# Weight fetches in eight paced pieces, first keys on another queue, and a new order of constants, in a fused attention and expert kernel

## The chip, the cores and the metric

The kernel runs on one core of a Trainium2 chip. The metric is the device time of one execution in microseconds (us): the median of the runs. A profile of one execution stands beside it, with a span of 499.8 us.

## What is computed

```
attention, batch 8, heads 12, sequence 448, head size 64:
  e    = exp(q k^T / 8 - max)
  attn = e / (sum(e) + exp(-max) + 1e-9)          # softmax with a one more in the sum
  x    = (attn v), laid out as 3584 tokens x 768
router, 8 experts: cosine of each token with each expert's embedding / tau
  expert = argmax, gate = softmax weight of that expert
expert MLP, per token:  out = gate * ( relu(x @ w1[expert]) @ w2[expert] )
  w1: 8 x 768 x 1024, w2: 8 x 1024 x 768, float32
```

## The kernel before, in words

The work is one long software pipeline, written out in `pipeline` (from L627). It counts in **steps**: step g (0 to 47) handles one pair of heads, six steps make one batch element b, and each step is cut into 8 slots (`NSLOT`). `put(slot, fn)` files a piece of work under a slot, and at the end all are emitted in order of slot. TensorE keeps this order exactly. On the other engines a scheduler places instructions by the order in which it expects their inputs, and the helper `behind(k, inst, other)` can tell it that one instruction has to come after another in the same engine's queue, which adds no semaphore.

For a pair of heads: queries and keys are loaded (`load_qk`, L166 to L171) and values too (`load_v`, L180 to L182), one group of twelve transfers on SyncE's queue for two steps, into three rotating sets of buffers. `front_q` and `front_k` transpose them on TensorE; VectorE copies the queries (L225), ScalarE the keys (L237). `front_v` (L246 to L254) puts the values into `vab` on GpSimd. `scores` multiplies (L268), takes the exponential on ScalarE (L273) and subtracts 1 on VectorE (L275). `attend` and `attend_rest` (L293, L306) multiply by the values; with them come the sums of the rows, which after every second step ScalarE's queue copies with a small transfer to the tile `den` (L317). `recip` inverts them, GpSimd spreads them over a tile with the constant `chunk` (L339), `normalise` brings them to all rows by a product with the constant `sel` (L350) and writes x.

After the six steps of a batch element the router runs. `router_pick` finds the expert with most tokens of this batch element and GpSimd loads its number into a register. `fetch` then loads that expert's weights, float32 in memory and bf16 in the tile, in four transfers from GpSimd's queue (L476), two halves of w1 and two of w2, from the pool `wp` with six buffers. Some four steps later `moe_chunks` spreads the expert's products over six steps: eight `moe_h` (L488), then seven of `moe_y` and `moe_yr` (L503, L518). Tokens that chose another expert are done in a loop at the end, if there are any.

Before the pipeline `build_consts` makes the constants that the first steps need. `build_late_consts`, in slot 2, makes `sel`, `chunk` (128 x 448, by eight selections on GpSimd, L98), an iota for the router and others. `warm` keeps TensorE busy with 48 products at the start, and with single ones in the first steps.

Buffers and semaphores: a buffer of a pool is filled again when its last reader is done. Each transfer of the SyncE and ScalarE queues signals its end on one of eight semaphores in turn, in the order the scheduler expects, and the program makes a transfer wait until the transfer eight earlier, which used the same semaphore, has landed.

Of the kernel before, what the change touches and what calls it, by code (L numbers as in the profile page):

```python
# [9 lines left out]
F32 = mybir.dt.float32  # L10
# [13 lines left out]
SM = 384  # L24
# [13 lines left out]
def build_consts(k):  # L38
    nc, pool = k.nc, k.const
    k.ident = pool.tile([128, 128], F32, name="ident")  # L40
    make_identity(nc, k.ident[:])
    k.ones_f = pool.tile([128, 1], F32, name="ones_f")
    nc.vector.memset(k.ones_f[:], 1.0)

    k.vld, k.krest, k.qrest, k.vab, k.rc, k.vst = [], [], [], [], [], []
    for s in range(NG):
        v = pool.tile([128, 2 * GP, 4, DH], F32, name=f"vld{s}")
        nc.gpsimd.memset(v[64:128, :, 3, :], 0.0)
        k.vld.append(v)
        kr = pool.tile([128, GP, 128], F32, name=f"krest{s}")  # L50
        nc.vector.memset(kr[:], 0.0)
        k.krest.append(kr)
        qr = pool.tile([128, 2 * GP, DH], F32, name=f"qrest{s}")
        nc.gpsimd.memset(qr[64:128, GP:, :], 0.0)
        k.qrest.append(qr)
    for s in range(2):
        va = pool.tile([128, 4, 4, 64], F32R, name=f"vab{s}")
        for h in range(2):
            nc.vector.tensor_copy(
                out=va[:, :, 2 * h + 1, :],  # L60
                in_=k.ones_f[:, 0:1].unsqueeze(2).broadcast_to([128, 4, 64]),
            )
        k.vab.append(va)
        rc = pool.tile([128, CN], F32R, name=f"rc{s}")
        nc.vector.memset(rc[:].bitcast(F32), 0.0)
        k.rc.append(rc)
        k.vst.append(pool.tile([128, NG, 4 * GP], F32, name=f"vst{s}"))


def build_late_consts(k):  # L70

    nc, pool = k.nc, k.const
    k.ones32 = pool.tile([128, 32], F32, name="ones32")
    nc.vector.memset(k.ones32[:], 1.0)
    k.ones_b = pool.tile([128, 128], BF16, name="ones_b")
    nc.vector.memset(k.ones_b[:], 1.0)


    sel_f = k.yp.tile([128, GP, 2, 64], F32, name="sel_f", tag="y")
    k.chunk = pool.tile([128, CH, CN], BF16, name="chunk")  # L80
    nc.gpsimd.memset(sel_f[:], 0.0)
    nc.vector.memset(k.chunk[:], 0.0)
    for base in (0, 64):
        r = sel_f[base : base + 2 * GP * CH]

        nc.gpsimd.affine_select(out=r, in_=r, compare_op=ALU.is_ge, fill=1.0, base=-1,
                                pattern=[[0, GP], [0, 2], [0, 64]], channel_multiplier=0)
        nc.gpsimd.affine_select(out=r, in_=r, compare_op=ALU.is_ge, fill=0.0, base=0,
                                pattern=[[-2 * CH, GP], [-CH, 2], [0, 64]], channel_multiplier=1)
        nc.gpsimd.affine_select(out=r, in_=r, compare_op=ALU.is_ge, fill=0.0, base=CH - 1,  # L90
                                pattern=[[2 * CH, GP], [CH, 2], [0, 64]], channel_multiplier=-1)
    k.sel = pool.tile([128, GP, 128], F32R, name="sel")
    nc.vector.tensor_copy(out=k.sel[:], in_=sel_f[:].rearrange("p g h d -> p g (h d)"))
    n = 2 * GP * CH
    for base in (0, 64):
        r = k.chunk[base : base + n]
        for i in range(2 * GP):
            nc.gpsimd.affine_select(out=r, in_=r, compare_op=ALU.not_equal, fill=1.0, base=-CH * i,  # L98
                                    pattern=[[-1, CH], [0, CN]], channel_multiplier=1)

    k.mask = pool.tile([128, 4, E], F32, name="mask")
    nc.vector.memset(k.mask[:], 1.0)
    nc.vector.memset(k.mask[64:128, 3, :], 0.0)
    k.ind = pool.tile([128, 4, 32], F32, name="ind")
    for i in range(4):
        nc.vector.reduce_sum(out=k.ind[:, i, :], in_=k.ident[:].rearrange("p (b c) -> p c b", c=32), axis=AX.X)
    k.half = pool.tile([128, 4], F32, name="half")
    nc.vector.memset(k.half[:], 0.5)
    iota_i = pool.tile([128, E], I32, name="iota_i")
    nc.gpsimd.iota(iota_i[:], pattern=[[1, E]], base=0, channel_multiplier=0)  # L110
    k.iota = pool.tile([128, E], F32, name="iota")
    nc.vector.tensor_copy(out=k.iota[:], in_=iota_i[:])
    k.rr = pool.tile([128, 512], F32, name="rr")
    nc.vector.memset(k.rr[:], 0.0)
    k.cnt_all = pool.tile([128, B, E], F32, name="cnt_all")
    k.oh0_all = pool.tile([128, B, E], F32, name="oh0_all")
    k.g_all = pool.tile([128, B, 4, E], F32, name="g_all")
    k.idx_all = pool.tile([128, B, 8], U32, name="idx_all")
# [32 lines left out]
def load_qk(k, n):  # L151
# [9 lines left out]
    def rest2(src, two):  # L161
        return src[b].rearrange("(g two) s d -> two s g d", two=2)[two, SM:S, g0 : g0 + GP, :]

    for dst, src in ((t.qm, k.q), (t.km, k.k)):
        for j in range(3):
            nc.sync.dma_start(  # L166
                dst[:, j, :, :], src[b, h0 : h0 + 2 * GP, 0:SM, :].rearrange("h (p t) d -> t p h d", t=3)[j]
            )
    nc.sync.dma_start(t.qr[0:64, :, :], k.q[b, h0 : h0 + 2 * GP, SM:S, :].rearrange("h p d -> p h d"))
    nc.sync.dma_start(t.kr[0:64, :, 0:64], rest2(k.k, 0))  # L170
    nc.sync.dma_start(t.kr[64:128, :, 64:128], rest2(k.k, 1))  # L171
    k.ld[n] = t


# [66 lines left out]
def front_v(k, g):  # L241
# [3 lines left out]
    for h in range(2):  # L245
# [5 lines left out]
        out=va[0:64, 3, 0, :], in0=t.v[0:64, 2 * i, 3, :],  # L251
        scalar1=1.0, scalar2=0.0, op0=ALU.mult, op1=ALU.add,
    )
    nc.gpsimd.tensor_scalar(  # L254
        out=va[64:128, 3, 2, :], in0=t.qr[64:128, i, :],
        scalar1=1.0, scalar2=0.0, op0=ALU.mult, op1=ALU.add,
    )
# [206 lines left out]
    k.e0[b], k.wts[b] = e0, ([], [])  # L464


def fetch(k, b, i):

    nc, e0 = k.nc, k.e0[b]
    if i < 2:  # L470
        w = k.wp.tile([128, NP, F // 2], BF16, name="w", tag="w")
        src = k.w1[bass.ds(e0, 1), :, :].rearrange("o (c p) f -> p (o c) f", p=128)[:, :, F // 2 * i : F // 2 * (i + 1)]
    else:
        w = k.wp.tile([128, 4, DM], BF16, name="w", tag="w")
        src = k.w2[bass.ds(e0, 1), :, :].rearrange("o (f p) m -> p (o f) m", p=128)[:, 4 * (i - 2) : 4 * i - 4, :]
    nc.gpsimd.dma_start(w[:], src)  # L476
    k.wts[b][i // 2].append(w)


def keep_xb(k, b):  # L480
# [3 lines left out]
def moe_h(k, xb, w1, f):  # L484
    nc = k.nc
    ps = k.work.tile([128, 512], F32, name="work", tag="work")
    for c in range(NP):
        nc.tensor.matmul(  # L488
            ps[:, 0:S], lhsT=w1[f // 4][:, c, 128 * (f % 4) : 128 * (f % 4) + 128], rhs=xb[:, c, :],
            start=(c == 0), stop=(c == NP - 1),  # L490
        )
    h = k.hp.tile([128, S], BF16, name="h", tag="h")
    nc.scalar.activation(h[:], ps[:, 0:S], ACT.Relu)  # L493
    return h


def moe_y(k, hs, w2, g0, t, n):
# [3 lines left out]
    ps = k.work.tile([128, 512], F32, name="work", tag="work")  # L501
    for f in range(NF):
        nc.tensor.matmul(  # L503
            ps[:, 0:SM], lhsT=hs[f][:, 128 * t : 128 * t + 128], rhs=w2[f // 4][:, f % 4, SM * n : SM * n + SM],
            start=(f == 0), stop=(f == NF - 1),
        )
    nc.vector.tensor_scalar_mul(yt[:], ps[:, 0:SM], g0[:, t : t + 1])  # L507
# [3 lines left out]
def moe_yr(k, hs, w2, g0):  # L511
# [4 lines left out]
    for f in range(NF):  # L516
        for n in range(2):
            nc.tensor.matmul(  # L518
                ps[64 * n : 64 * n + 64, 0:SM], lhsT=hs[f][:, SM:S], rhs=w2[f // 4][:, f % 4, SM * n : SM * n + SM],
                start=(f == 0), stop=(f == NF - 1),  # L520
            )
    nc.vector.tensor_scalar_mul(yt[:], ps[:, 0:SM], g0[:, 3:4])
# [29 lines left out]
def other_experts(k):  # L552
# [13 lines left out]
    with tc.If(any_ > 0):  # L566
# [6 lines left out]
        with tc.For_i(0, B * E, 1) as i:  # L573
# [3 lines left out]
            with tc.If(n > 0):  # L577
# [3 lines left out]
                g = p.tile([128, 4], F32, name="gx", tag="gx")  # L581
                nc.sync.dma_start(g[:], k.g_dram.rearrange("b e p t -> (b e) p t")[bass.ds(i, 1)].rearrange("o p t -> p (o t)"))
                nc.vector.tensor_copy(out=g[64:128, 3:4], in_=g[0:64, 3:4])
                w1, w2 = [], []
                for j in range(2):
                    w = k.wp.tile([128, NP, F // 2], BF16, name="w", tag="w")
                    nc.gpsimd.dma_start(
                        w[:],
                        k.w1[bass.ds(e, 1), :, :].rearrange("o (c p) f -> p (o c) f", p=128)[:, :, F // 2 * j : F // 2 * (j + 1)],
                    )  # L590
                    w1.append(w)
                for j in range(2):
                    w = k.wp.tile([128, 4, DM], BF16, name="w", tag="w")
                    nc.gpsimd.dma_start(
                        w[:], k.w2[bass.ds(e, 1), :, :].rearrange("o (f p) m -> p (o f) m", p=128)[:, 4 * j : 4 * j + 4, :]
                    )
                    w2.append(w)
                hs = [moe_h(k, xb, w1, f) for f in range(NF)]
                r0 = b * S
                for t in range(3):  # L600
# [28 lines left out]
def pipeline(k):  # L629
# [4 lines left out]
    def put(slot, fn):  # L634
        at.setdefault(slot, []).append(fn)

    put(2, lambda: build_late_consts(k))
    put(12, lambda: prep_expert_emb(k, k.emb, k.tau))
    put(5 * NSLOT, lambda: prep_expert_emb_t(k))
    for n in range(NG * B):  # L640
# [26 lines left out]
    for b in range(B):  # L667
# [1 line left out]
        put(s, lambda b=b: router_mm(k, b))  # L669
        put(s + 4, lambda b=b: router_tok(k, b))  # L670
        put(s + 7.6, lambda b=b: router_pick(k, b))
        for i, o in enumerate((7.6, 7.6, 9, 18)):
            put(s + o, lambda b=b, i=i: fetch(k, b, i))
        put(s + 14, lambda b=b: keep_xb(k, b))
        put(s + 9, lambda b=b: router_exp(k, b))
        put(s + 14, lambda b=b: router_act(k, b))
# [12 lines left out]
def kernel(  # L689
# [39 lines left out]
    n.xbp = pool("xbp", 3)  # L729
    n.rp = pool("rp", 1)  # L730
    n.g0p = pool("g0p", 3)
    n.wp = pool("wp", 6)
    n.hp = pool("hp", 10)
    n.yp = pool("yp", 3)
    n.ld, n.qts, n.kts, n.ems, n.nbs, n.den, n.va, n.sv = {}, {}, {}, {}, {}, {}, {}, {}
# [40 lines left out]
```

The softmax here doesn't subtract the row's maximum and nothing guards it: scores larger than these inputs give would overflow.

## Time and profile before

| | |
|---|---|
| time, median of 2 runs | 504.06 us (503.33 to 504.8) |
| span of the profiled run | 499.8 us |
| TensorE busy (matmul) | 407.9 us, 82% |
| VectorE, ScalarE, GpSimd busy | 324.1, 273.6, 198.5 us |
| weights transfers | 32 of 768 KB, 13.6 us from issue to landing (median) |
| all transfers | 76.24 MB |

How to read it. The page cuts the span into 40 slices of 12.5 us; each digit is a busy share in tenths. PEclk is the granted clock of TensorE, 9 for full. The share of the transfer engines can exceed 1 in the stage tables[...]. A line of the timeline gives the start, the duration, the engine, the source line, the operation and its tiles, how many were merged, and in brackets how long the engine had been idle and what ended it. SPq and ACTq are the queues of SyncE and ScalarE while they issue transfers. Where several things were waited for, the profile names the one that came last.

### The profile page before, as it was taken

The page shows a single profiled execution, that of the slowest core. Times are in us where ns is not written, and L with a number is a line of the kernel's source. Part 1 is how long each engine was busy: PE and PEld are TensorE (multiplying, and loading weights), DVE is VectorE, ACT ScalarE, POOL GpSimd, SP SyncE. Part 2 cuts the span into 40 slices and gives each one's busy share as a digit, 9 for nine tenths or more (in the row PEclk, how much of TensorE's full clock was granted, in tenths as well). Part 3 has the DMA queues.
Part 4 walks back from the last instruction along what each step waited for, and adds up shares of the span by engine and source line. Part 5 has one row for each costly group of instructions (what it writes and reads, how often), then busy time and mean ns, then how long its engine had stood idle before and what let it go on. Part 6 is the DMA issues. An engine that isn't in the chain of part 4 may idle for free.

```text
span 499.8 us, 7648 instructions
## 1 busy us (share of the span) xinstructions
PE 407.9 (82%) x2392; PEld 248.7 (50%) x2392; DVE 324.1 (65%) x810; ACT 273.6 (55%) x419; POOL 198.5 (40%) x365
## 2 busy tenths in 40 slices
PE   6378688764999399975999399975999499979986
PEld 4245454433566265643565265643565265543533
DVE  3267688893698376874688376874698386864203
ACT  1277476753786267843786267843786277713130
POOL 5665344563356125443356225443356232401200
PEclk9698789995999789997999789997999799999989
DMA  6844436499529956698729966698729911891983
GB/s 158 185 113 114 115 77 194 71 198 220 143 46 195 220 162 170 101 201 222 210 44 192 223 162 168 103 200 214 217 46 194 205 64 57 133 230 59 174 190 112
DMA packets 144204, 76.24 MB, mean 153 GB/s; under 512 B 103193, under 2 KB 143129, under 8 KB 144161
## 3 DMA queue, kind: packets, MB, share of 16 engines
q1 hardware_dynamic: 120336, 44.87, 38.3%
q0 software_dynamic: 22144, 30.67, 32.8%
q10 hardware_dynamic: 1680, 0.17, 0.3%
q8 instruction: 20, 0.33, 0.3%
q14 instruction: 24, 0.19, 0.1%
HBM read 84.17 MB, written 16.52 MB: 201 GB/s over the span
## 4 chain that ended last, share of the span: by engine, by line
PE 56%; DMA 22%; DVE 5%; POOL 5%; ACT 4%; issue 4%; SPq 2%; ACTq 1%; POOLq 0%; DVEq 0%
PE work L488 12%; PE big L293 11%; DMA vld<-in_v_dram 7%; DMA den<-nb 6%; PE work L503 6%; PE big L268 6%; PE work L380 4%; DMA qrest<-in_q_dram 4%; PE big L306 3%; ACT e L273 3%; PE work L222 3%; PE work L350 2%; DMA out_dram<-y 2%; PE work L518 2%; PE work L234 2%
## 5 line engine op out<-in xcount | busy, mean ns | idle before, releaser
L273 ACT ACTIVATE e<-big 128x896 f32<-128x896 f32 x144 | 128.2, 920 | 25.8 <-PE big L268 20.9
L275 DVE TENSOR_SCALAR em<-e 128x896 fp32r<-128x896 f32 x144 | 94.9, 659 | 36.9 <-ACT e L273 35.9
L268 PE MATMUL big<-qt,kt 64*128 64x448 f32 x288 | 54.5, 431 | 60.0 <-ACT kt L237 48.6
L488 PE MATMUL work<-xb,w 128*128 128x448 bf16 x384 | 85.2, 363 | 2.4 <-DVE y L507 2.4
L293 PE MATMUL big<-em,vab 128*128 128x448 f32 x288 | 76.5, 404 | 6.8 <-ACT e L273 5.3
L246 POOL TENSOR_SCALAR vab<-vld 128x192 fp32r<-128x192 f32 x96 | 38.6, 416 | 107.5 <-PE big L293 99.8
L313 ACT COPY nb<-big 128x896 f32<-128x896 f32 x48 | 43.5, 906 | 58.7 <-PE big L306 58.7
L503 PE MATMUL work<-w,h 128*128 128x384 bf16 x384 | 74.4, 345 | 0.1
L507 DVE TENSOR_SCALAR y<-work,g 128x384 f32<-128x384 f32 x48 | 29.4, 612 | 64.7 <-DMA out_dram<-y 42.5
L355 DVE SCALAR_TENSOR_TENSOR x<-nb,sv,work 64x448 f32<-64x448 f32 x96 | 64.9, 676 | 5.0 <-PE work L350 3.4
L293 PEld LDWEIGHTS big<-em,vab 128*128 128x128 f32 x288 | 57.7, 205 | 15.7 <-ACT e L273 6.8
L237 ACT CAST kt<-work 128x512 fp32r<-128x512 f32 x48 | 28.2, 588 | 67.5 <-DMA vld<-in_v_dram 38.5
L268 PEld LDWEIGHTS big<-qt,kt 64*128 64x128 f32 x288 | 25.8, 204 | 74.9 <-ACT kt L237 52.3
L488 PEld LDWEIGHTS <-w 128*128 128x128 bf16 x384 | 35.7, 101 | 39.4 <-issue 15.1
L493 ACT ACTIVATE h<-work 128x448 bf16<-128x448 f32 x64 | 34.9, 545 | 36.4 <-PE work L488 36.2
L503 PEld LDWEIGHTS <-h 128*128 128x128 bf16 x384 | 38.0, 102 | 30.7 <-issue 11.6
L191 POOL TENSOR_TENSOR vs<-vld 128x256 f32<-128x256 f32 x24 | 18.7, 780 | 66.5 <-DMA vld<-in_v_dram 57.1
L225 DVE CAST qt<-work 128x448 fp32r<-128x448 f32 x48 | 29.9, 623 | 15.4 <-PE work L223 14.7
L476 POOL DMA_DIRECT2D w<-in_moe_w_dram x32 | 26.6, 841 | 30.9 <-DVE x L355 25.8
L339 POOL TENSOR_TENSOR rt<-rc,chunk 128x448 fp32r<-128x448 f32 x24 | 25.2, 1049 | 34.4 <-DVE rc L337 32.9
L282 DVE TENSOR_SCALAR emx<-e 128x448 fp32r<-128x448 f32 x48 | 21.5, 447 | 14.0 <-ACT e L280 13.8
L350 PE MATMUL work<-rt,sel 128*128 128x448 f32 x48 | 22.3, 464 | 9.3 <-POOL rt L339 5.9
(113 smaller groups left out, 581.3 us busy)
## 6 DMA issues: line engine op xcount, KB each, us to landing
w<-in_moe_w_dram POOLq DMA_DIRECT2D x32, 768.0 KB, 13.6
qm<-in_q_dram SPq DMA_DIRECT2D x72, 128.0 KB
km<-in_k_dram SPq DMA_DIRECT2D x72, 128.0 KB
vld<-in_v_dram SPq DMA_DIRECT2D x24, 384.0 KB
out_dram<-y SPq DMA_DIRECT2D x48, 192.0 KB
xb_dram<-xb POOLq DMA_DIRECT2D x8, 672.0 KB, 5.3
qrest<-in_q_dram SPq DMA_DIRECT2D x24, 64.0 KB
krest<-in_k_dram SPq DMA_DIRECT2D x48, 32.0 KB
```

The lines of the kernel that those rows point to most:

```text
L225: nc.vector.tensor_copy(out=qt[:], in_=ps[:, 0:S])
L246: nc.gpsimd.tensor_scalar(out=va[:, 0:3, 2 * h, :], in0=t.v[:, 2 * i + h, 0:3, :], scalar1=1.0, scalar2=0.0, op0=ALU.mult, op1=ALU.add,)
L268: nc.tensor.matmul(ps[:, h, 0:S], lhsT=kt[64 * h : 64 * h + 64, 128 * j : 128 * j + 128], rhs=qt[64 * h : 64 * h + 64, :], start=True, sto ...
L273: k.last_e = nc.scalar.activation(e[:], ps[:, :, 0:S], ACT.Exp, scale=scale)
L275: k.last = nc.vector.tensor_scalar_sub(em[:], e[:], 1.0)
L293: nc.tensor.matmul(ps[:, h, 0:S], lhsT=va[:, j, 2 * h : 2 * h + 2, :], rhs=k.ems[g, j][:, h, :], start=(j == 0), stop=False,)
L313: nc.scalar.copy(out=nb[:, i, :, :], in_=ps[:, :, 0:S])
L350: nc.tensor.matmul(ps[:, 0:S], lhsT=k.sel[:, g % GP, :], rhs=rt[:].rearrange("p c n -> p (c n)"), start=True, stop=True)
L355: nc.vector.scalar_tensor_tensor(out=x[r, :], in0=nb[0:64, g % GP, h, :], scalar=k.sv[b][:, 2 * c + h : 2 * c + h + 1], in1=ps[r, 0:S], op ...
L488: nc.tensor.matmul(ps[:, 0:S], lhsT=w1[f // 4][:, c, 128 * (f % 4) : 128 * (f % 4) + 128], rhs=xb[:, c, :], start=(c == 0), stop=(c == NP ...
L493: nc.scalar.activation(h[:], ps[:, 0:S], ACT.Relu)
L503: nc.tensor.matmul(ps[:, 0:SM], lhsT=hs[f][:, 128 * t : 128 * t + 128], rhs=w2[f // 4][:, f % 4, SM * n : SM * n + SM], start=(f == 0), st ...
```

## The change

Three things are changed. The weights of a batch element are fetched in eight pieces of half the size, and each piece is put, by `behind`, after the last `front_v` instruction of its step in GpSimd's queue (`k.last_v`), over six steps; the pool gets ten buffers of half the size. This is meant to spread the transfers over time. The keys of the very first group of heads are loaded through ScalarE's queue beside the queries on SyncE's. The late constants are emitted one slot later, iota is made early, `chunk` is first built narrow and then widened by VectorE, and the copies of `sel` and `chunk` on VectorE are put behind the first scores; this is meant to let the first steps begin before the constants are made.

```diff
 def build_consts(k):
+    iota_i = pool.tile([128, E], I32, name="iota_i")
+    nc.gpsimd.iota(iota_i[:], pattern=[[1, E]], base=0, channel_multiplier=0)
+    k.iota = pool.tile([128, E], F32, name="iota")
+    nc.vector.tensor_copy(out=k.iota[:], in_=iota_i[:])
...
 def build_late_consts(k):
-    k.chunk = pool.tile([128, CH, CN], BF16, name="chunk")
+    ch_f = k.yp.tile([128, CH], F32, name="ch_f", tag="y")
-    nc.vector.memset(k.chunk[:], 0.0)
+    nc.gpsimd.memset(ch_f[:], 0.0)
...
-    nc.vector.tensor_copy(out=k.sel[:], in_=sel_f[:].rearrange("p g h d -> p g (h d)"))
+    behind(k, nc.vector.tensor_copy(out=k.sel[:], in_=sel_f[:].rearrange("p g h d -> p g (h d)")), k.last)
...
-                                    pattern=[[-1, CH], [0, CN]], channel_multiplier=1)
+                                    pattern=[[-1, CH]], channel_multiplier=1)
+    k.chunk = pool.tile([128, CH, CN], BF16, name="chunk")
+    behind(k, nc.vector.tensor_copy(out=k.chunk[:], in_=ch_f[:].unsqueeze(2).broadcast_to([128, CH, CN])), k.last)
...
-    iota_i = pool.tile([128, E], I32, name="iota_i")
-    nc.gpsimd.iota(iota_i[:], pattern=[[1, E]], base=0, channel_multiplier=0)
-    k.iota = pool.tile([128, E], F32, name="iota")
-    nc.vector.tensor_copy(out=k.iota[:], in_=iota_i[:])
...
 def load_qk(k, n):
-    for dst, src in ((t.qm, k.q), (t.km, k.k)):
+    keng = nc.sync if n else nc.scalar
+    for eng, dst, src in ((nc.sync, t.qm, k.q), (keng, t.km, k.k)):
         for j in range(3):
-            nc.sync.dma_start(
+            eng.dma_start(
...
-    nc.sync.dma_start(t.kr[0:64, :, 0:64], rest2(k.k, 0))
-    nc.sync.dma_start(t.kr[64:128, :, 64:128], rest2(k.k, 1))
+    keng.dma_start(t.kr[0:64, :, 0:64], rest2(k.k, 0))
+    keng.dma_start(t.kr[64:128, :, 64:128], rest2(k.k, 1))
...
 def front_v(k, g):
-    nc.gpsimd.tensor_scalar(
+    k.last_v = nc.gpsimd.tensor_scalar(
...
+def w_piece(k, e0, i):
+    if i < 4:
+        w = k.wp.tile([128, NP, F // 4], BF16, name="w", tag="w")
+        src = k.w1[bass.ds(e0, 1), :, :].rearrange("o (c p) f -> p (o c) f", p=128)[:, :, F // 4 * i : F // 4 * (i + 1)]
+    else:
+        w = k.wp.tile([128, 2, DM], BF16, name="w", tag="w")
+        src = k.w2[bass.ds(e0, 1), :, :].rearrange("o (f p) m -> p (o f) m", p=128)[:, 2 * i - 8 : 2 * i - 6, :]
+    return w, k.nc.gpsimd.dma_start(w[:], src)
+
 def fetch(k, b, i):
-    if i < 2:
-        w = k.wp.tile([128, NP, F // 2], BF16, name="w", tag="w")
...
-    nc.gpsimd.dma_start(w[:], src)
-    k.wts[b][i // 2].append(w)
+    w, inst = w_piece(k, k.e0[b], i)
+    behind(k, inst, k.last_v)
+    k.wts[b][i // 4].append(w)
...
 def pipeline(k):
-    put(2, lambda: build_late_consts(k))
+    put(3, lambda: build_late_consts(k))
...
-        for i, o in enumerate((7.6, 7.6, 9, 18)):
-            put(s + o, lambda b=b, i=i: fetch(k, b, i))
+        for i, o in enumerate((1, 1, 2, 3, 4, 4, 5, 6)):
+            put(((b + 1) * NP + 3 + o) * NSLOT + 7.7, lambda b=b, i=i: fetch(k, b, i))
...
-    n.wp = pool("wp", 6)
+    n.wp = pool("wp", 10)
```

`moe_h`, `moe_y` and `moe_yr` take the pieces by new indices (`w1[f // 2]`, `w2[f // 2]`), and the loop at the end uses `w_piece` too.

More of the change, by code (lines that the diff above doesn't have):

```diff
@@ L92, in build_late_consts @@
     k.sel = pool.tile([128, GP, 128], F32R, name="sel")
-    nc.vector.tensor_copy(out=k.sel[:], in_=sel_f[:].rearrange("p g h d -> p g (h d)"))
+    behind(k, nc.vector.tensor_copy(out=k.sel[:], in_=sel_f[:].rearrange("p g h d -> p g (h d)")), k.last)
     n = 2 * GP * CH
     for base in (0, 64):
-        r = k.chunk[base : base + n]
+        r = ch_f[base : base + n]
         for i in range(2 * GP):
             nc.gpsimd.affine_select(out=r, in_=r, compare_op=ALU.not_equal, fill=1.0, base=-CH * i,
-                                    pattern=[[-1, CH], [0, CN]], channel_multiplier=1)
+                                    pattern=[[-1, CH]], channel_multiplier=1)
+    k.chunk = pool.tile([128, CH, CN], BF16, name="chunk")
+    behind(k, nc.vector.tensor_copy(out=k.chunk[:], in_=ch_f[:].unsqueeze(2).broadcast_to([128, CH, CN])), k.last)
     k.mask = pool.tile([128, 4, E], F32, name="mask")
@@ L464, in router_pick @@
     k.e0[b], k.wts[b] = e0, ([], [])
-def fetch(k, b, i):
-    nc, e0 = k.nc, k.e0[b]
-    if i < 2:
-        w = k.wp.tile([128, NP, F // 2], BF16, name="w", tag="w")
[L472 to L475, printed above, removed]
-    nc.gpsimd.dma_start(w[:], src)
-    k.wts[b][i // 2].append(w)
+def w_piece(k, e0, i):
[6 more added lines that the diff above has]
+    return w, k.nc.gpsimd.dma_start(w[:], src)
+def fetch(k, b, i):
+    w, inst = w_piece(k, k.e0[b], i)
+    behind(k, inst, k.last_v)
+    k.wts[b][i // 4].append(w)
 def keep_xb(k, b):
@@ L488, in moe_h @@
         nc.tensor.matmul(
-            ps[:, 0:S], lhsT=w1[f // 4][:, c, 128 * (f % 4) : 128 * (f % 4) + 128], rhs=xb[:, c, :],
+            ps[:, 0:S], lhsT=w1[f // 2][:, c, 128 * (f % 2) : 128 * (f % 2) + 128], rhs=xb[:, c, :],
             start=(c == 0), stop=(c == NP - 1),
@@ L503, in moe_y @@
         nc.tensor.matmul(
-            ps[:, 0:SM], lhsT=hs[f][:, 128 * t : 128 * t + 128], rhs=w2[f // 4][:, f % 4, SM * n : SM * n + SM],
+            ps[:, 0:SM], lhsT=hs[f][:, 128 * t : 128 * t + 128], rhs=w2[f // 2][:, f % 2, SM * n : SM * n + SM],
             start=(f == 0), stop=(f == NF - 1),
@@ L518, in moe_yr @@
             nc.tensor.matmul(
-                ps[64 * n : 64 * n + 64, 0:SM], lhsT=hs[f][:, SM:S], rhs=w2[f // 4][:, f % 4, SM * n : SM * n + SM],
+                ps[64 * n : 64 * n + 64, 0:SM], lhsT=hs[f][:, SM:S], rhs=w2[f // 2][:, f % 2, SM * n : SM * n + SM],
                 start=(f == 0), stop=(f == NF - 1),
@@ L583, in other_experts @@
                 nc.vector.tensor_copy(out=g[64:128, 3:4], in_=g[0:64, 3:4])
[L584 to L597, printed above, removed]
+                w = [w_piece(k, e, j)[0] for j in range(8)]
+                w1, w2 = w[:4], w[4:]
                 hs = [moe_h(k, xb, w1, f) for f in range(NF)]
```

## The prediction

> **What bounds the kernel now.** I read the granted clock and transfer rows of the page first, then the chain of waits, then the timeline and the stage table around one batch.
>
> ```profile
> PEclk9698789995999789997999789997999799999989
> DMA  6844436499529956698729966698729911891983
> GB/s 158 185 113 114 115 77 194 71 198 220 143 46 195 220 162 170 101 201 222 210 44 192 223 162 168 103 200 214 217 46 194 205 64 57 133 230 59 174 190 112
> ```
>
> The transfer engines fill up once per batch (a 9 every four or five slices), then rest, and the clock dips with it. The fetches of weights stand at 203.98 and 259.66 us, so a batch takes 55.7 us. One batch by stages (columns: PE, PEld, DVE, ACT, POOL busy, clock, DMA share, GB/s):
>
> ```profile
> 208.00:210.00 2.00, 2.00 (x13) 1.56 (x11) 1.46 (x4) 1.37 (x2) 0.95 (x2) 1.00 1.21 196
> 224.00:226.00 2.00, 0.00 (x0) 0.00 (x0) 0.00 (x0) 0.00 (x0) 0.00 (x0) 1.00 1.17 217
> 228.00:230.00 2.00, 0.00 (x0) 0.00 (x0) 0.00 (x0) 0.00 (x0) 0.68 (x1) 0.50 0.88 253
> 232.00:234.00 2.00, 2.00 (x9) 1.04 (x7) 1.78 (x4) 1.22 (x2) 0.00 (x0) 0.57 1.08 242
> 234.00:278.00 44.00, 43.32 (x275) 27.16 (x274) 35.79 (x90) 30.50 (x47) 21.22 (x39) 1.00 0.74 155
> ```
>
> In the last row TensorE is busy 43.3 of 44 us at full clock: there it is the bound. Around 222 to 230 us everything stands still but the transfers, and TensorE restarts at half clock. Who stands there, in the timeline of SyncE's queue and of ScalarE:
>
> ```profile
> 204.17 1.48 SPq L166 DMA_DIRECT2D qm<-in_q_dram  x3
> 205.74 6.67 SPq L166 DMA_DIRECT2D km<-in_k_dram  x3
> 212.45 4.37 SPq L169 DMA_DIRECT2D qrest<-in_q_dram  x1
> ...
> 219.44 0.92 ACT L273 ACTIVATE e<-big 128x896 f32<-128x896 f32 x1
> 229.23 0.80 ACTq L317 DMA_DIRECT2D den<-nb  x1
> 230.07 0.59 ACT L237 CAST kt<-work 128x512 fp32r<-128x512 f32 x1 [9.71 <-DMA vld<-in_v_dram]
> ```
>
> Three loads that issue in 1.5 us at 204 take 6.7 us right after, because four weight transfers were issued between 203.98 and 209. ScalarE then cannot issue the small `den` transfer (L317): in the built program it waits for a completion semaphore that it shares with the load eight issues earlier, here the `vld` load, landed at 229.15. In order behind it stands the copy of the keys, and behind that TensorE's scores. So the stall is a queue of four: weights burst, loads late, `den` issue held, ScalarE held. The other two `den` issues of a batch (204.47, 243.43) wait for nothing.
>
> The start has a second one:
>
> ```profile
> 11.23 0.27 PE L235 MATMUL work<-ident,krest 128*128 128x128 f32 x1
> 19.18 0.17 DVE L112 CAST iota<-iota_i 128x8 f32<-128x8 int32 x1 [5.32 <-POOL iota_i L110]
> 19.26 0.62 DVE L225 CAST qt<-work 128x448 fp32r<-128x448 f32 x1
> 20.03 1.12 PE L268 MATMUL big<-qt,kt 64*128 64x448 f32 x4 [8.52 <-DVE qt L225]
> ```
>
> The transposed queries are in PSUM at 11.1, but VectorE copies them only at 19.26, behind an iota that GpSimd makes after all its late constants.
>
> **What the Trainium skill says.** "DMA: Bandwidth & Descriptors", section "Queues, rings and completion order": each transfer engine takes its queues in turn, a packet at a time. So a weight queue with work takes a share from the loads for as long as it lasts; the 6.67 us above against 1.56 us at 231 us agree. Same page, "Issuing engines are not separate DMA queues": a second issuing engine saves only issue time. "TensorE: Matmul & The Clock Gate", section on the HAM clock gate: half clock after an idle window of about 3.4 us, full again after as long a busy one. Here TensorE stops at 222.8, falls to 0.50 near 226.9 and is back near 233.7, 3 us after its restart: agrees. First page again, "Specifications": under 512 B a transfer loses line rate. The new pieces of w1 write rows of just 512 B (256 values of bf16); no trace here shows them.
>
> **The change part by part.**
>
> *Paced weights.* Per batch eight pieces of 384 KB take the place of four of 768 KB, each ordered behind the `front_v` work of its step, from the late half of step 6b+10 to that of 6b+15. The ordering is on GpSimd's own queue and adds no semaphore. A piece at the 196 GB/s of the 208 to 210 row takes 0.393 MB / 196 = 2.0 us where a batch's burst takes 16. So SyncE's group of twelve loads (issue 7 us, landed some 9 us after its start) comes at most some 4 us later when two pieces run beside it: 13 us. The `den` that stalled is issued 219.55 - 204.17 = 15.4 us after the group's start. It fits, so this wait should go.
>
> What goes with it, from the table of TensorE's idle time us by us: idle 9.0, 8.1, 7.9, 7.9, 7.5 and 6.7 us after the first six fetches, together 47.1. After them TensorE is busy 5.5, 5.0, 3.0, 5.3, 3.6 and 3.3 us at half clock, 25.7 us, of which half, 12.9, is lost at most; I take 10, since some of it is latency between engines that the clock doesn't touch. The slow `den` at the head of the burst (6.5 us) also leaves TensorE short by 0.5 to 0.8 us once a batch (213, 269, 326, 381 us): 3 in all.
>
> The fetches of the last two batches have no `front_v` left to stand behind: b=6 all follow the last one, b=7 none. They stay bursts; I take nothing for them.
>
> *Cost of the pieces.* GpSimd issues eight transfers of 0.83 us (median of L476) instead of four: +3.3 us a batch. It is busy about 22 of 46 us and waits for TensorE before most `front_v`; hidden. Weights late? Piece 3 is issued at step 12.5 for use at 16.6, the last at 15.5 for 17.1; a step is 7.7 us, so 12 us at least for a transfer of 2 to 6. Ten buffers of half size replace six: piece j reuses a buffer that the batch before freed a step or more earlier. Hidden.
>
> *Load on the transfer engines.* A batch moves weights 3.15 MB at 196 GB/s (16 us), q, k, v 4.13 MB at the 228 of 10 to 11 us (18), output 1.38 MB at the 257 to 283 of 236 to 240 us (5) and the kept activations 0.69 MB at 330 (2): 41 us in a period of about 46. If 512 B rows cost nothing it stays 41; if half of the weights (w1) took twice as long, 49. I take the lower end with 1 us of new waits per batch, 6 in all, since 41 of 46 leaves little room.
>
> *Start.* Iota moves ahead of the other constants, `sel` and `chunk` go behind the first scores, and `chunk` is built 14 columns wide instead of 448. VectorE is then free at 5.6. Keys on ScalarE's queue take 5 issues of about 0.55 us from SyncE, so q, k and v land 2 to 3 us sooner; the activation table (1.28 us) is then loaded behind these issues, by 6 us, before ScalarE has other work. But TensorE's 48 warming products end at 9.07 either way; q, k and kt need 1.9 us more (8.8 to 10.0 for the transposes, 0.6 and 0.3 for copy and release): scores at 11.0 instead of 20.03, 9.0 us. The clock stood at 0.50 from 15.6 to 25.6; without the gap it should hold, which I count as 1.5. The two copies moved into step 0 on VectorE cost 0.3 + 0.5 us beside ScalarE's exponentials: hidden.
>
> **Sum.** 504.06 - 47.1 - 10 - 3 + 6 - 9.0 - 1.5 = 439.5; I forecast 440 us. The steady batch becomes 55.7 - 7.5 - 1.7 - 0.6 + 1 = about 47.
>
> **Rivals.**
>
> *Transfers become the bound.* Rows of 512 B cost double: 49 us per batch and some unevenness, 51. Then 4.7 saved per batch instead of 9 to 10: 504 - 6 x 4.7 - 10.5 = 465. For it: 1.21 in the share column during a burst. Against: w1 keeps 512 B, just not under the skill's limit.
>
> *The `den` wait stays at half.* The loads still land late because out writes and two pieces meet: 4 us of idle per batch, and no fall of the clock since that needs longer. 504 - 6 x 5.5 - 10.5 = 460.
>
> *Slower.* With the rests gone, TensorE's clock falls lastingly to 0.8: 46.3 / 0.8 = 57.9 us per batch, 504 + 6 x 2.2 - 5 = 512. Against: 44 us without a rest at 1.00 from 234 to 278.
>
> *Better than forecast.* No new waits, all half-clock time won: 440 - 6 - 3 = 431.
>
> **How the numbers follow.** Forecast 440 with 0.55, better 0.20, `den` at half 0.12, transfers 0.10, slower 0.03. Range 427 to 465: the upper end takes in the two middle rivals, the lower one the better case with some of the last bursts. Everything but the last rival is over 2% faster: faster 0.95, same 0.02, slower 0.03.
>
> **What would show it.** Right: first scores of L268's successor at 11 us; no `den` issue that starts 9 us after ScalarE's work before it; TensorE never idle 3 us between 15 us and the end of attention; clock at 1.00 there; fetches of successive batches 46 to 48 us apart. Wrong: transfer share near 1 throughout with TensorE waiting for `w`; a wait of POOL for its own transfers ahead of `vab`; ScalarE still released by a load; or a clock under 1.00 in a busy stretch.

## The result, and the profile after

The changed kernel takes **458.28 us** (median of 2 runs, 457.54 to 459.03) against 504.06: a ratio of 0.909 (95% interval 0.901 to 0.918), 45.8 us less. The forecast was 440 us with a range of 427 to 465. So the direction and the range held, and the point was 18 us too low. The span of the profiled run is 457.2 us.

The same three rows of the page as before (40 slices of 11.4 us now), and the rows of the weight queue and of two VectorE groups (from the page's parts 2, 3 and 5):

```profile
PEclk9859998988999989999999989998999999989989
DMA  9964556399969988899969999999979764973973
GB/s 175 183 154 111 127 124 176 72 167 188 218 126 201 172 210 179 149 204 199 238 119 200 182 203 191 156 215 208 204 125 199 141 139 63 202 182 72 208 166 123
...
q0 software_dynamic: 34944, 30.68, 42.9%
...
L278 DVE TENSOR_SCALAR em<-e 128x896 fp32r<-128x896 f32 x144 | 106.8, 745 | 32.3 <-ACT e L276 31.5
L514 DVE TENSOR_SCALAR y<-work,g 128x384 f32<-128x384 f32 x48 | 29.2, 609 | 41.9 <-DMA out_dram<-y 26.3
```

The rhythm of full and empty slices of transfers has gone, and after the 5 in the third slice, which belongs to the start, the clock falls no lower than 8. Three of these 8s (slices 15, 24 and 28) lie where TensorE paused, as shown below, and the last row gives the first hint why: VectorE stood 26.3 us in all waiting for an output tile `y` to be sent away.

The clearest measure is the distance between the first router products of successive batch elements (line L383 in the new kernel, L380 in the old):

| starts of the router's products, us | distances |
|---|---|
| before: 81.17, 133.52, 190.47, 246.14, 302.92, 358.50, 413.26 | 52.4, 57.0, 55.7, 56.8, 55.6, 54.8 |
| after: 73.35, 119.80, 171.24, 221.97, 272.85, 323.69, 370.10 | 46.5, **51.4, 50.7, 50.9, 50.8**, 46.4 |

Two of the six batches after are as long as forecast ("about 47"). The four between them are 4.5 us longer than these two, 18.2 us in all, which is the size of the miss. Each of the four has a pause of TensorE in it, of 3.6, 1.6, 2.2 and 3.0 us, and each pause ends when VectorE gets its `y` tile. Here is the second batch by stages (columns: PE, PEld, DVE, ACT, POOL busy, clock, DMA share, GB/s):

```profile
158.00:160.00 2.00, 2.00 (x11) 0.99 (x11) 0.49 (x1) 1.46 (x2) 0.72 (x2) 1.00 0.99 162
160.00:164.00 4.00, 0.41 (x4) 0.04 (x1) 0.71 (x2) 0.00 (x0) 0.00 (x0) 0.98 1.10 228
164.00:168.00 4.00, 4.00 (x14) 2.93 (x15) 3.91 (x8) 2.22 (x4) 1.16 (x4) 0.59 0.72 217
168.00:212.00 44.00, 42.43 (x270) 25.97 (x269) 34.98 (x89) 30.86 (x49) 23.93 (x43) 1.00 0.92 173
```

It is the same picture as the stall of before at half its length: 3.6 us with nothing but transfers, then half clock. Who stands there, in the timeline of the same stretch:

```profile
150.90 0.58 DVE L514 TENSOR_SCALAR y<-work,g 128x384 f32<-128x384 f32 x1
151.08 4.50 SPq L169 DMA_DIRECT2D km<-in_k_dram  x3
...
157.08 0.60 SPq L174 DMA_DIRECT2D krest<-in_k_dram  x1
157.78 1.01 SPq L548 DMA_DIRECT2D out_dram<-y  x2
...
163.29 0.62 DVE L514 TENSOR_SCALAR y<-work,g 128x384 f32<-128x384 f32 x1 [4.80 <-DMA out_dram<-y]
163.97 0.74 PE L353 MATMUL work<-rt,sel 128*128 128x448 f32 x1 [3.59 <-DVE y L514]
...
164.89 0.92 ACT L276 ACTIVATE e<-big 128x896 f32<-128x896 f32 x1 [5.00 <-DVE emx L285]
```

The tile written at 150.90 is sent only at 157.78, because SyncE first issues the loads of queries and keys that stand ahead of it in its queue. There are three `y` buffers, and two more tiles are written before 155.2. So VectorE's next `y` waits until 163.29, when the first of the three has landed. In order behind it stands everything else that VectorE does for the attention, and TensorE and ScalarE wait for that. This wait isn't about `den`; no line of the prediction speaks of `y` as a buffer.

**It could have been read before.** The waits of the kernel before have it, next to the one that the prediction used:

```profile
DVE y L507 <- DMA out_dram<-y: 42.5, 9, 7.8
ACT kt L237 <- DMA vld<-in_v_dram: 38.5, 4, 9.9
```

(engine and line, what released it: us in total, times, the longest.) The timeline of the very stall that the prediction took apart has both, 0.06 us from each other:

```profile
230.01 0.62 DVE L507 TENSOR_SCALAR y<-work,g 128x384 f32<-128x384 f32 x1 [7.56 <-DMA out_dram<-y]
230.07 0.59 ACT L237 CAST kt<-work 128x512 fp32r<-128x512 f32 x1 [9.71 <-DMA vld<-in_v_dram]
```

So it is in four of the six stalls before (173, 230, 286 and 342 us): the two waits end within 0.3 us of each other. They lie in the second to fifth batch, and these are the four that stay long after the change.

**The start** of the changed kernel, in its timeline:

```profile
11.45 0.67 PE L271 MATMUL big<-qt,kt 64*128 64x448 f32 x4 [0.68 <-ACT kt L240]
...
20.21 0.39 DVE L105 CAST chunk<-ch_f 128x448 bf16<-128x448 f32 x1 [2.34 <-POOL ch_f L102]
20.52 0.39 DVE L285 TENSOR_SCALAR emx<-e 128x448 fp32r<-128x448 f32 x1
...
21.00 0.92 ACT L276 ACTIVATE e<-big 128x896 f32<-128x896 f32 x1 [4.13 <-DVE emx L285]
...
21.06 0.74 PE L309 MATMUL big<-emx,vab 64*128 64x448 f32 x2 [2.60 <-DVE emx L285]
```

The first scores come at 11.45 instead of 20.03. But `chunk` now lies on VectorE ahead of `emx` of step 0, and waits for GpSimd's selections; TensorE, which needs `emx`, rests 2.6 us until 21.06, and between 21 and 34 us it works at half clock:

```profile
21.00:34.00 13.00, 11.82 (x41) 7.93 (x41) 7.97 (x14) 7.70 (x10) 7.39 (x14) 0.50 0.66 159
```

At the first router product 7.8 of the 8.6 us are still there. Whether the rest brings on the half clock is another question; e2 and e6 below bear on it.

### The profile page after: what moved, and what is told of

Read it like the earlier page. It is cut to its first block, busy times and chain, and to the rows that moved or that the text cites. A ratio compares the mean times of both kernels' runs of the same rounds, so it can differ in the third digit from the quotient of the medians.

```text
span 457.2 us, 7738 instructions
## 1 busy us (share of the span) xinstructions
PE 406.7 (89%) x2392; PEld 247.1 (54%) x2392; DVE 333.0 (73%) x810; ACT 275.1 (60%) x419; POOL 213.5 (47%) x398
## 3 DMA queue, kind: packets, MB, share of 16 engines
q0 software_dynamic: 34944, 30.68, 42.9%
## 4 chain that ended last, share of the span: by engine, by line
PE 49%; DVE 18%; DMA 11%; issue 6%; POOL 5%; ACT 4%; SPq 0%; ACTq 0%; POOLq 0%; DVEq 0%
PE work L495 12%; PE big L296 10%; DMA out_dram<-y 7%; PE work L510 6%; DVE em L278 5%; PE big L271 5%; PE work L383 4%; PE big L309 3%; DMA krest<-in_k_dram 3%; ACT e L276 3%; DVE x L358 3%; POOL rt L342 3%; PE work L353 2%; PE work L225 2%; DVE qt L228 2%
## 5 line engine op out<-in xcount | busy, mean ns | idle before, releaser
L278 DVE TENSOR_SCALAR em<-e 128x896 fp32r<-128x896 f32 x144 | 106.8, 745 | 32.3 <-ACT e L276 31.5
L249 POOL TENSOR_SCALAR vab<-vld 128x192 fp32r<-128x192 f32 x96 | 36.3, 389 | 132.8 <-PE big L296 105.0
L510 PE MATMUL work<-w,h 128*128 128x384 bf16 x384 | 68.7, 327 | 0.0
L296 PEld LDWEIGHTS big<-em,vab 128*128 128x128 f32 x288 | 56.7, 202 | 16.0 <-ACT e L276 8.5
L514 DVE TENSOR_SCALAR y<-work,g 128x384 f32<-128x384 f32 x48 | 29.2, 609 | 41.9 <-DMA out_dram<-y 26.3
L478 POOL DMA_DIRECT2D w<-in_moe_w_dram x64 | 52.0, 816 | 15.8 <-PE work L510 5.3
L271 PE MATMUL big<-qt,kt 64*128 64x448 f32 x288 | 52.1, 412 | 7.6 <-ACT kt L240 4.1
L500 ACT ACTIVATE h<-work 128x448 bf16<-128x448 f32 x64 | 34.8, 544 | 38.8 <-PE work L495 38.6
L510 PEld LDWEIGHTS <-h 128*128 128x128 bf16 x384 | 35.9, 98 | 26.0 <-issue 5.4
L353 PE MATMUL work<-rt,sel 128*128 128x448 f32 x48 | 22.9, 476 | 19.9 <-DVE y L514 10.4
L271 PEld LDWEIGHTS big<-qt,kt 64*128 64x128 f32 x288 | 24.8, 194 | 21.9 <-issue 6.9
L194 POOL TENSOR_TENSOR vs<-vld 128x256 f32<-128x256 f32 x24 | 17.6, 735 | 28.9 <-issue 28.6
L371 ACT ACTIVATE xs<-x 128x448 f32<-128x448 f32 x48 | 27.7, 577 | 3.4 <-DVE x L358 3.4
```

The costliest lines, as they stand in the source:

```text
L249: nc.gpsimd.tensor_scalar(out=va[:, 0:3, 2 * h, :], in0=t.v[:, 2 * i + h, 0:3, :], scalar1=1.0, scalar2=0.0, op0=ALU.mult, op1=ALU.add,)
L271: nc.tensor.matmul(ps[:, h, 0:S], lhsT=kt[64 * h : 64 * h + 64, 128 * j : 128 * j + 128], rhs=qt[64 * h : 64 * h + 64, :], start=True, sto ...
L278: k.last = nc.vector.tensor_scalar_sub(em[:], e[:], 1.0)
L296: nc.tensor.matmul(ps[:, h, 0:S], lhsT=va[:, j, 2 * h : 2 * h + 2, :], rhs=k.ems[g, j][:, h, :], start=(j == 0), stop=False,)
L478: return w, k.nc.gpsimd.dma_start(w[:], src)
L510: nc.tensor.matmul(ps[:, 0:SM], lhsT=hs[f][:, 128 * t : 128 * t + 128], rhs=w2[f // 2][:, f % 2, SM * n : SM * n + SM], start=(f == 0), st ...
```

## The experiments

The ratios are taken against runs of the kernel before that were made beside each of them (medians of 502.2 to 504.1 us), so they differ a little from the quotient of two times in the table.

| run | what it is | us | ratio to before (95%) |
|---|---|---|---|
| changed kernel | | 458.28 | 0.909 (0.901 to 0.918) |
| e1 | before, with the paced pieces alone | 469.64 | 0.931 (0.924 to 0.938) |
| e2 | before, with the start alone | 493.92 | 0.983 (0.977 to 0.988) |
| e3 | changed, six y tiles | 440.79 | 0.875 (0.869 to 0.882) |
| e4 | before, six y tiles | 502.67 | 1.001 (0.999 to 1.004) |
| e5 | changed, long rows of w1 | 455.7 | 0.905 (0.899 to 0.911) |
| e6 | changed, late constants later still | 461.96 | 0.917 (0.910 to 0.925) |
| e7 | before, den issued by GpSimd, six y tiles | 527.62 | 1.048 (1.041 to 1.055) |
| e8 | before, den issued by GpSimd | 527.03 | 1.046 (1.040 to 1.053) |
| e9 | changed, six y tiles, four paced halves | 439.44 | 0.875 (0.872 to 0.879) |
| e10 | changed, six y tiles, long rows | 438.61 | 0.870 (0.868 to 0.873) |

### Each part alone (e1, e2)

e1 is the kernel before with `w_piece`, the paced `fetch` and the ten buffers; e2 is the kernel before with the edits of the start.

```diff
 # e1: of the change, only
+            put(((b + 1) * NP + 3 + o) * NSLOT + 7.7, lambda b=b, i=i: fetch(k, b, i))
 # e2: of the change, only
+    keng = nc.sync if n else nc.scalar
...
+    put(3, lambda: build_late_consts(k))
```

> The kernel before with the eight paced pieces alone; constants and the first keys as before. The two parts of the change touch different stretches, so they should add up: the change as a whole gave 45.8 us, and the first router product came 7.8 us earlier (73.4 against 81.2 us), which is what the new start gave. Theory: 466 us, first scores at 20 us, fetches of successive batches 51 us apart. Rival (the parts depend on each other, since an earlier start makes the loads and the pieces collide): under 460 or over 472.

> The kernel before with the new start alone (constants reordered, first keys on ScalarE's queue); weights in four pieces in one burst. Theory: 496 to 498 us, that is 7 us faster, first scores near 11.4 us, and the six stalls of about 8 us still there, one per batch, with ScalarE released by a load. Rival (the start is worth what the forecast said, 10.5 us): 493.5.

Measured: 469.64 and 493.92 us. The first lies between the 466 of its theory and the rival's "over 472"; the second is the rival's 493.5, not the 496 to 498 of the theory. By the ratios the pieces give 0.0692 and the start 0.0175 of 504 us, 34.9 and 8.8 us, together 43.7; both at once gave 45.8. Within the intervals (31 to 38 us, and 6 to 12) the parts add up. The forecast had 54.1 for the pieces (47.1 + 10 + 3 - 6) and 10.5 for the start, so the miss is the pieces': 19 of them against 2.

The profile of e2 also shows that the half clock near the start is not tied to the rest that ends at 21 us. The start is that of the changed kernel, but the clock is down before that moment, and hardly after it:

```profile
11.00:21.00 10.00, 8.61 (x30) 5.35 (x29) 3.82 (x9) 5.28 (x7) 8.36 (x23) 0.55 0.88 185
21.00:34.00 13.00, 8.21 (x47) 5.10 (x46) 9.20 (x17) 8.60 (x12) 8.37 (x16) 0.95 0.77 179
```

Its first router product starts at 70.81, 10.4 us earlier than before, where the changed kernel has 73.35. All six profiles with this start (changed kernel, e2, e3, e5, e9, e10) have it between 70.8 and 73.4.

### Six output tiles instead of three (e3, e4)

The theory: before, VectorE's wait for `y` lay beside ScalarE's wait for its `den` issue, and cost nothing; the paced pieces ended the second and left the first as the longest. Three more `y` buffers should then do nothing for the kernel before, and give the missing 18 us to the changed one.

```diff
-    n.yp = pool("yp", 3)
+    n.yp = pool("yp", 6)
```

> The changed kernel with six output tiles y in place of three. In the changed kernel VectorE waits 26 us in all until an output transfer has freed a tile, and TensorE stands still behind it (3.6, 1.6, 2.2 and 3.0 us after 160, 213, 263 and 313 us, and then runs some us at half clock). Theory (the y tiles are the wait that took the place of the old one): these pauses go and the batch shortens from 51 to 48 us; 443 to 447 us. Rival (the transfer engines are the bound and the wait only moves to loads or weights): 455 to 458 us.

> The kernel before with six output tiles y in place of three. There VectorE waits 42.5 us in all for output transfers, in the same stalls in which ScalarE is held at its small den transfer. Theory (ScalarE's held den transfer is what stops TensorE, the y wait lies beside it): no gain, 500 to 504 us, ScalarE still released by a load after some 9 us. Rival (the y tiles were the stall before as well): 460 to 470 us.

Measured: 440.79 for the changed kernel, below the 443 to 447 of its theory, and 502.67 for the one before, a ratio of 1.001, as its theory had it. The same edit is worth 17 us in one (0.909 - 0.875 of 504) and nothing in the other. The row for `y` in the waits of e3:

```profile
DVE y L514 <- PE work L510: 22.1, 13, 12.5
```

VectorE waits only for the product now, never for the transfer. The router's products of e3 start at 72.89, 119.37, 165.95, 212.57, 258.70, 305.82 and 352.30: every batch takes 46.1 to 47.1 us. In the stage tables over the inner part of the attention, before (first line) and in e3 (second):

```profile
40.00:430.00 390.00, 325.75 (x1918) 201.06 (x1918) 277.96 (x683) 240.45 (x369) 166.99 (x301) 0.91 0.72 152
...
46.00:370.00 324.00, 307.95 (x1874) 190.32 (x1875) 276.37 (x663) 235.00 (x361) 172.69 (x315) 0.98 0.91 179
```

TensorE's busy share rises from 84% at a clock of 0.91 to 95% at 0.98. In e4, VectorE's wait for the output is gone in the same way, but the wait of ScalarE stands as it stood:

```profile
ACT kt L237 <- DMA vld<-in_v_dram: 39.2, 4, 10.1
```

So both waits were there side by side. That the `den` wait alone kept the batch long under the burst is shown by e4; that the `y` wait alone kept it 4.5 us longer under the pieces, by e3. What the `y` wait alone would cost under the burst no run shows, and that both waits come from the burst (loads and outputs late behind it) is read from the timeline.

### The `den` wait taken away without the pieces (e7, e8)

The other side of the same question: if `den` can't hold ScalarE, but the weights still come in a burst, does the `y` wait take its place? GpSimd issues `den` instead, whose transfers don't share ScalarE's semaphores.

```diff
-        nc.scalar.dma_start(den[:], nb[64:65, :, :, :].rearrange("p i h s -> p (i h s)"))
+        nc.gpsimd.dma_start(den[:], nb[64:65, :, :, :].rearrange("p i h s -> p (i h s)"))
```

> The kernel before, weights in one burst, with the small den transfer issued by GpSimd in place of ScalarE and with six y tiles in place of three. Theory (the stall was two waits side by side on late transfers, ScalarE held by the issue of den and VectorE by the y tiles; with both taken away the burst itself costs little): 445 to 462 us. Rival (late loads or a late den are themselves needed by then, whatever holds the engines): 485 us or more.

> The kernel before with the small den transfer issued by GpSimd in place of ScalarE, three y tiles as before. Theory (two waits side by side): VectorE's wait for a y tile, 42.5 us in all before, now holds TensorE alone and for nearly as long: 485 to 502 us. Rival (the held ScalarE was the whole stall): 445 to 465 us, as without the y wait.

Measured: 527.62 and 527.03 us, slower than before. For e7 that is the rival's side ("485 us or more", a late `den` is itself needed by then); for e8 it is outside both ranges. ScalarE no longer waits for a load, but in e7:

```profile
POOL rt L339 <- DVE rc L337: 87.4, 9, 13.2
DVE den L333 <- DMA den<-nb: 67.2, 7, 11.4
```

The transfer of 7 KB now lies in the queue of the weights, behind a burst of them: it lands 3.8 us after its issue in the median and up to 17.7. Before, VectorE waited 4.9 us in all for `den`, not 67.2, so this lateness is the edit's own. VectorE's wait for `y` is only 8.2 us in e8, while the pipeline is slowed at `den`. So these two runs put a new wait in place of the old, and don't answer the question. The side-by-side theory rests on e3, e4 and the timelines.

### The rows of 512 B (e5)

The weight queue's time rose from 32.8% of 499.8 us to 42.9% of 457.2, 164 to 196 us, 4 us a batch, where the prediction took nothing. e5 cuts w1 by input rows, three pieces with rows of 2 KB, in seven pieces a batch and nine buffers.

```diff
-    if i < 4:
-        w = k.wp.tile([128, NP, F // 4], BF16, name="w", tag="w")
+    if i < 3:
+        w = k.wp.tile([128, 2, F], BF16, name="w", tag="w")
...
-            ps[:, 0:S], lhsT=w1[f // 2][:, c, 128 * (f % 2) : 128 * (f % 2) + 128], rhs=xb[:, c, :],
+            ps[:, 0:S], lhsT=w1[c // 2][:, c % 2, 128 * f : 128 * f + 128], rhs=xb[:, c, :],
```

> The changed kernel with w1 cut along its 768 rows instead of its 1024 columns: three pieces of 512 KB whose rows are 2 KB in the tile, in place of four with 512 B; w2 as in the changed kernel, nine buffers of 4 KB. The share of the weight queue rose with the change from 32.8% of 499.8 us to 42.9% of 457.2 us, that is from 164 to 196 us of all engines, 4 us a batch. Theory (short rows cost transfer time, and that makes output transfers late): weight queue back at 160 to 165 us, VectorE's wait for y tiles under 15 us in all, 449 to 453 us. Rival (rows of 512 B cost nothing on the path): 456 to 460 us.

Measured: 455.7 us, at the rival's edge (456 to 460) and not the theory's 449 to 453; the intervals of this run and of the changed kernel overlap. The queue (packets, MB, share of 452.8 us):

```profile
q0 software_dynamic: 16384, 30.67, 38.1%
```

172.5 us, some 24 less than 196. The rows cost transfer time, as the prediction's upper end had it in part (4 of the 8 us a batch), but no gain in the kernel's time can be told: the wait for `y` is still 27.8 us in e5, where the theory had under 15.

### The constants out of step 0 (e6)

Does the half-clock stretch at the start come from the pause at 18 to 21 us? e6 puts the late constants eight slots later, into step 1.

```diff
-    put(3, lambda: build_late_consts(k))
+    put(11, lambda: build_late_consts(k))
```

> The changed kernel with the late constants filed under slot 11 instead of 3, so that GpSimd makes them after the values of step 1, and VectorE copies them in step 1 or 2 and not ahead of the first emx. In the changed kernel TensorE stands from 18.5 to 21.0 us behind them and then runs at half clock until 34.9 us. Theory: no pause there, 453 to 455 us. Rival (another wait of the first steps holds as long): 457 to 460 us.

Measured: 461.96 us, no gain, and above even the rival's 457 to 460. The pause at 18 to 21 is gone, but GpSimd's selections now stand ahead of its sums of the values, and VectorE waits for these (`vt`) with a later copy of the queries in order behind it:

```profile
18.13 2.38 POOL L102 TENSOR_SCALAR_AFFINE_SELECT ch_f<-ch_f 56x14 f32<-56x14 f32 x8
...
22.97 0.45 DVE L204 STREAM_TRANSPOSE vt<-vs 128x256 f32<-128x256 f32 x1 [4.33 <-POOL vs L196]
...
25.05 1.02 PE L271 MATMUL big<-qt,kt 64*128 64x448 f32 x4 [1.82 <-DVE qt L228]
```

The clock is 0.53 on average from 11 to 21.6 us and 0.72 from 21.6 to 34. But e2, with the constants where the changed kernel has them, also has 0.55 from 11 to 21, so the earlier fall is not shown to be e6's doing. In both places that were tried GpSimd's constants held up another engine. What sets the clock in the first 35 us stays open.

### What of the pieces counts (e9), and the two repairs together (e10)

e9 goes back to four fetches of 768 KB, but paced like the pieces, on six y tiles; e10 joins e3 and e5.

```diff
 # e9, against the kernel of e3
-        for i, o in enumerate((1, 1, 2, 3, 4, 4, 5, 6)):
+        for i, o in enumerate((1, 2, 4, 5)):
...
-    n.wp = pool("wp", 10)
+    n.wp = pool("wp", 6)
```

> The changed kernel with six output tiles y, and with the weights in four paced halves of 768 KB instead of eight quarters (behind the same value work, at steps 10, 11, 13 and 14 of a batch, six buffers), so rows of w1 are 1 KB again. Separates the pacing from the number of pieces. Theory 'what counts is that a piece does not arrive in the middle of the burst with three others; the number of pieces is free': 4 us of two halves one behind the other in the weight queue is what a group of loads can bear, so the den issue of ScalarE stays unheld and the time is that of the six-tile kernel, 438 to 444 us; transfers of the weight queue back near 165 to 175 us. Rival 'the small pieces matter, a half of 768 KB in the middle of a group of loads makes it late': pauses of ScalarE behind a load come back, 2 to 4 us a batch, 452 to 465 us.

> The changed kernel with six output tiles y and with w1 cut by input rows into three pieces of 2 KB rows (seven pieces a batch, nine buffers). Theory 'with the wait for y gone TensorE is the bound and the transfers have room, so a cheaper weight queue buys nothing': 438 to 442 us, 0.870 to 0.880. Rival 'the 24 us of transfer time that the longer rows save are partly on the path once the y tiles are not': 434 to 437 us, below 0.868.

Measured: 439.44 and 438.61 us. Both hit their theory. Four paced halves are as good as eight paced quarters, so with six `y` tiles the cutting isn't needed for the gain; the pacing is what the two have in common. Eight pieces in a burst, cutting without pacing, were not run. And once TensorE is busy 95% of the time, a weight queue with 22 us less to do (39.2% of 433.7 = 170.0 us, against 43.9% of 438.5 = 192.5 in e3) shows no gain that can be told: the intervals of e3 and e10 overlap. All three beat the kernel before and the changed one.

## Why the prediction was right or wrong

**The queue of four: right.** The pieces end the burst, the loads come in time, and ScalarE is held before `den` only once, at 203.05, for 1.4 us of TensorE's time. What was right most closely is the time of a batch: "about 47" against 46.1 to 47.1 us wherever no `y` wait falls in, and the 10 us for half clock is in that. Two readings on the way there were loose. The sum for the batch takes off 7.5 us of idle time, where its own six figures average 7.85. And 219.55 is the moment when the source of `den` was ready; the issue came at 229.23. Neither moves the result.

**The step that failed: "I take the lower end with 1 us of new waits per batch, 6 in all".** The direction and the mechanism of the removed wait were right; this term was mis-sized. It was the term in which every wait behind the removed one had to go, and it was filled from the load on the transfer engines alone. The wait that took over was known by name in the profile of before: VectorE's for `y`, 42.5 us, released within 0.06 us of ScalarE's in the stall that was taken apart. It kept four batches at 51.0 instead of 46.4 us, and six tiles took off 17 us. Without it (e3) the kernel takes 440.79, the forecast itself with its 6 us of new waits. So the 17 us come on top of the 6 and are nearly the whole miss of 18: by this count the term should have been about 23. That e3 meets 440 so closely is in part luck, since the start gave less than its term.

**What fell with it.** Of the signs that were to show the steps right, "TensorE never idle 3 us between 15 us and the end of attention" and "clock at 1.00 there" did not come: the four pauses are 3.6, 1.6, 2.2 and 3.0 us long, and after all but the one of 1.6 the clock is at 0.57 to 0.59 for a stretch of 4 us. One sign of being wrong came: a clock under 1.00 in a busy stretch, 0.50 from 21 to 34 us with TensorE busy for 11.8 of 13. The rival with `den` at half took 4 us of idle time as too short for the clock to fall, and the prediction elsewhere about 3.4 us as what a fall needs; here a pause of 2.2 us was followed by half clock, and the measurement decides. Neither of the two middle rivals was right either: `den` didn't stay at half, and TensorE didn't wait for `w`. The time came near theirs (460 and 465) by another cause, which shows how little a total tells. The range reached up to 465 for their sake, so that it held 458 is luck.

**The transfer load: the wrong end, without harm.** "If 512 B rows cost nothing it stays 41": they cost 4 us a batch. That made the load 45 of 46 us by the prediction's sum. In e3 the share of the transfer engines from 46 to 370 us is 0.91; since this share goes over 1 in bursts (1.21 before), it doesn't say how near a bound is. TensorE is at 95% there, and e5 and e10 gain nothing that can be told from lighter transfers.

**GpSimd and late weights: right, with room to spare.** GpSimd is busy 213.5 instead of 198.5 us, and no wait of TensorE for `w` stands in the list of waits after. But a piece takes 7.5 us from issue to landing in the median, not the "2 to 6" that the prediction allowed; the 196 GB/s behind its 2.0 us is what all queues moved together. The 12 us of slack held it.

**The start: 9.0 + 1.5 forecast, 8.8 measured alone** (6 to 12 by its interval, so the total can't tell the two apart). The first scores are right to half a microsecond (11.0 against 11.45). The clock did not hold: in all six profiles with this start its mean from 10 to 35 us is 0.73 to 0.80, though the place of the half clock differs. "The two copies moved into step 0 on VectorE ... hidden" left out that the copies also *wait*, for GpSimd, 2.34 us at `chunk`, and that `emx` stands behind them. By e6, moving them doesn't help.

**The bursts of the last two batch elements: right.** TensorE still rests 3.2 us until 404.84 and 2.7 us until 436.41, against 3.1 and 2.4 in the same two places before. As forecast, nothing is gained there.

## What to carry to other kernels

When a burst of transfers holds several engines at once, list every wait that ends in the same microsecond, not only the one on the chain: when the first is removed, the next can stand in its place. Ask then of each buffer that the late transfers free (loads, outputs, small copies) whether its pool bridges the group of loads that stands ahead in the issuing queue; a deeper pool that is worth nothing today can be worth more than a third of the change tomorrow (17 us of 46 here). Price a wait that an edit moves along with its instruction, not the instruction alone.

## What the runs showed of the hardware

**Casting transfers in rows of 512 B.** The same 30.7 MB of weights took 164 us of the transfer engines' time in 22,144 packets (before), 196 in 34,944 (rows of 512 B in half of them, changed), 192.5 in as many (e3), 172.5 and 170 in 16,384 (e5, e10) and 170 in 22,144 (e9, 38.8% of 437.0). Among the paced kernels with six `y` tiles, rows of 512 B in w1 took 192.5 us and rows of 1 or 2 KB 170, some 22 us less; from 1 KB to 2 KB nothing was gained. The rows read from memory, in float32, are twice as long and change along, so the runs don't tell which side the cost belongs to. The Trainium skill, "DMA: Bandwidth & Descriptors", section "Specifications", has full rate from 512 B on; the measurement decides that these rows of just 512 B already cost more than rows of 1 KB. Shorter ones were not run.

**VectorE beside GpSimd.** The same `em` instruction took 659 ns in the mean before and 745 after; the median is 627 and 628, so it is some of them. Sorted by what GpSimd did at the same time (from 40 to 380 us): in the changed kernel 0.63 us for 76 of them beside neither kind of work, 0.90 for 20 that overlap the issue of a weight transfer, 0.92 for 31 that overlap a product or sum of two tiles; before, 0.62 for 84, 0.79 for 11 and 0.78 for 19. The Trainium skill, "SBUF — State Buffer", section "SBUF: two separate sides", says that VectorE, in modes that use two ports, and GpSimd share a pair of ports that one instruction holds to its end while the other stands still. The longer times agree in kind; that `em` runs in such a mode is not shown by a trace, and 16 of the 76 overlap GpSimd's copies into `vab` and are no longer for it, which fits the lock only if `em` had the ports first. In all, `em` takes 12 us more of VectorE's time after the change, and whether any of it lies on the path was not tested. The issues are not the main part: e9, with half as many, still has 735 ns, with only 3 of its `em` beside an issue and 43 beside GpSimd's work on two tiles, at 0.93.
